# Seven products of sums for the gate/value matmuls of an mLSTM and SwiGLU kernel, in an order that a list scheduler writes

## The chip, the cores and the metric

The kernel runs on one core of a Trainium2 chip. The metric is the device time of one execution in microseconds (us). Five engines work side by side and meet at semaphores: TensorE (PE; its weight loads are listed as PEld), VectorE (DVE), ScalarE (ACT), GpSimd (POOL) and SyncE (SP), which here issues nearly all transfers. Each engine takes its instructions in program order.

## The reference

An mLSTM cell runs over 4 batches x 8 heads x 768 steps with head dimension 40. Its output, seen as 3072 tokens x 320 features, goes through a SwiGLU feed-forward block with 1536 hidden features. All in float32:

```python
for t in range(S):                                  # S = 768
    m_new = np.maximum(f[:, :, t] + m, i[:, :, t])
    f_stab, i_stab = np.exp(f[:, :, t] + m - m_new), np.exp(i[:, :, t] - m_new)
    m = m_new
    C = f_stab[..., None, None] * C + i_stab[..., None, None] * np.einsum('bhd,bhe->bhde', vt, kt)
    n = f_stab[..., None] * n + i_stab[..., None] * kt
    denom = np.maximum(np.abs(np.einsum('bhd,bhd->bh', n, qt)[..., None]), 1.0)
    y[:, :, t] = sigmoid(o_gate[:, :, t]) * np.einsum('bhde,bhe->bhd', C, qt) / denom
x = y.transpose(0, 2, 1, 3).reshape(3072, 320)
g = x @ w_gate                                      # 320 x 1536
out = (g * sigmoid(g) * (x @ w_val)) @ w_out        # 1536 x 320
```

## The kernel before, in words

The 768 steps are cut in six groups of 128. A group holds the 128 steps of all four batches, 512 tokens, and goes through three things: the cell (here always one group ahead), the gate/value products with the SwiGLU product, and the output projection. In the code g counts from 0, so "groups 3 to 6" are g = 2 to 5; group 2 is g = 1. The cell for group g + 1 runs inside group g's gate/value tiles; the last group, g = 5, has no cell to do.

**Gate/value.** `hidden(g, m)` makes one of 12 tiles of 128 hidden features. The transposed inputs `xT_sb` hold the 320 features as five chunks of 64 rows, twice: the upper 64 partitions feed the gate product and the lower 64 the value product, so that the two halves of TensorE's rows work at the same time. Line 651 issues, per chunk, one matmul of 64 rows x 128 features x 512 tokens for each half. ScalarE takes Silu of the gate's bank (`sg`, L656), VectorE multiplies by the value's bank into `h_sb` (L657). Float32 matmuls leave two records each in the trace.

**Cell.** Its steps stand in `slots[m]`, and are issued after tile m: `do_scores` (L331) and `do_weigh` after tiles 3 and 4, `do_add` (L353) and `do_state` after tile 5, `do_attend` (`inter` L377, `intra` L382) with `do_gather` for the two halves of the heads after tiles 7 and 9, `do_divide` after 8 and 10. `gather` makes `y_sb` and `den` on VectorE (L391, L394, then L396 to L398 on 16 columns); `gate` multiplies `o_sb` by it on GpSimd (L403); `divide` multiplies by 1/den on VectorE into `x_sb` (L409). `send_squares` (L422) moves x to `x_sq` in 32 transfers so that VectorE's 32x32 transpose (`turn_inputs`, L426) can write `xT_sb` while the projection runs. q and k come in the same way, 16 transfers each (`load_squares`, L315), into `q_sq` and a `k_sq` of its own. The weights of the next group (`weights_sub` L451, `weights_mask` L456, `weights_exp` L460, `sig` L463, `weigh_values` L341) are made during the projection.

**Projection.** In groups 2 to 6 `project_seven` already multiplies two 2x2 block matrices with seven products: halves of the tokens and of the hidden features against halves of `wo_sb`, with sums of inputs made by GpSimd (`out_sums`, L689 to L691) and of weights (`out_weights`, once). Each product is 12 matmuls of 128 x 128 x 160 columns (L717). Group 1 uses the plain `project_all` (L668).

**Order.** What runs when is written out by hand: tile m, its sums, its slot, and steps between the products of the projection. PSUM's eight banks rotate in two pools of four ("gen" for products, "cell" for the cell).

Of the kernel before, what the change touches and what calls it, by code (L numbers as in the profile page):

```python
# [9 lines left out]
F32 = mybir.dt.float32  # L10
# [8 lines left out]
L = 128  # L19
SUB = 64  # L20
NEG = -1e30


@with_exitstack
def kernel(
# [34 lines left out]
    NH = NFC + 1  # L60
# [6 lines left out]
    work = ctx.enter_context(tc.tile_pool(name="work", bufs=2))  # L67
    psum = ctx.enter_context(tc.tile_pool(name="psum", bufs=4, space=PSUM))
    early_scope = ExitStack()
    early = early_scope.enter_context(tc.tile_pool(name="early", bufs=1))  # L70
# [18 lines left out]
    k_sb = const.tile([128, BH, DP], F32)  # L89
# [7 lines left out]
    x_sb = const.tile([128, B, DM + HP], F32)  # L97
# [4 lines left out]
    h_sb = const.tile([128, NH, TW], F32)  # L102
# [3 lines left out]
    ident = const.tile([128, 128], F32)  # L106
# [498 lines left out]
    piece_load(3, h_sb[:, NH - NKC:])  # L605
# [68 lines left out]

    KH = NFC // 2
    NW = DM // 2
    TH = TW // 2
    first_half, second_half = slice(0, TH), slice(TH, TW)

    def out_weights(eng):  # L680
        lo, hi = wo_sb[:, 0:KH], wo_sb[:, KH:]
        n1, n2 = slice(0, NW), slice(NW, DM)
        eng.tensor_tensor(wT[:, 0], lo[:, :, n2], lo[:, :, n1], op=ALU.subtract)
        eng.tensor_tensor(wT[:, 1], hi[:, :, n2], wT[:, 0], op=ALU.subtract)
        eng.tensor_tensor(wT[:, 2], hi[:, :, n1], wT[:, 1], op=ALU.subtract)
        eng.tensor_tensor(lo[:, :, n2], hi[:, :, n2], lo[:, :, n2], op=ALU.subtract)

    def out_sums(k, eng):
        eng.tensor_tensor(S1[:, k], h_sb[:, k, second_half], h_sb[:, KH + k, second_half], op=ALU.add)  # L689
        eng.tensor_tensor(h_sb[:, k, second_half], h_sb[:, k, first_half], h_sb[:, k, second_half], op=ALU.subtract)  # L690
        eng.tensor_tensor(S2[:, k], S1[:, k], h_sb[:, k, first_half], op=ALU.subtract)  # L691

    def out_fourth(eng):
        for k in range(0, KH, 2):
            a12 = h_sb[:, KH + k:KH + k + 2, first_half]
            eng.tensor_tensor(a12, a12, S2[:, k:k + 2], op=ALU.subtract)

    def project_seven(g, before):
        n1, n2 = slice(0, NW), slice(NW, DM)
        a11 = lambda k: h_sb[:, k, first_half]  # L700
        a12 = lambda k: h_sb[:, KH + k, first_half]
        a21 = lambda k: h_sb[:, k, second_half]
        a22 = lambda k: h_sb[:, KH + k, second_half]
        node = {x: bank("o_ps", "gen")[:, 0:DM].rearrange("p (u d) -> p u d", d=NW) for x in "eacdb"}
        kept = {x: work.tile([128, TW], F32, name="sg")[:, 0:DM].rearrange("p (u d) -> p u d", d=NW) for x in "uv"}

        def send(z, u, n):
            for i in range(2):
                nc.sync.dma_start(out=out[ds((u + i) * S + g * L, L), n], in_=z[:, i])

        def fresh():
            return work.tile([128, DM], F32, name="z_sb").rearrange("p (u d) -> p u d", d=NW)

        def product(x, lhs, rhs, start, stop):
            for k in range(KH):
                for i in range(2):
                    nc.tensor.matmul(node[x][:, i], lhsT=lhs(k)[:, ts(i, L)], rhs=rhs(k), start=start and k == 0 and i == 0,  # L717
                                     stop=stop and k == KH - 1, skip_group_check=True)

        def step(n):  # L720
            for f in before.get(n, ()):
                f()

        u2, v = kept["u"], kept["v"]
        step(0)
        product("e", a12, lambda k: wo_sb[:, KH + k, n1], True, True)
        step(1)
        product("a", a11, lambda k: wo_sb[:, k, n1], True, True)
        nc.scalar.copy(u2, node["a"])  # L729
        z = fresh()  # L730
        nc.vector.tensor_tensor(z, u2, node["e"], op=ALU.add)  # L731
        send(z, 0, n1)
        out_fourth(nc.vector)
        step(2)
        product("c", a21, lambda k: wo_sb[:, k, n2], True, False)
        nc.scalar.copy(v, node["c"])
        step(3)
        product("d", lambda k: S1[:, k], lambda k: wT[:, 0, k], True, False)
        nc.vector.tensor_tensor(v, v, node["d"], op=ALU.add)
        step(4)  # L740
        product("b", lambda k: S2[:, k], lambda k: wT[:, 1, k], True, True)
        nc.vector.tensor_tensor(u2, u2, node["b"], op=ALU.add)
        nc.gpsimd.tensor_tensor(v, v, u2, op=ALU.add)
        send(v, 2, n2)
        step(5)
        product("c", a22, lambda k: wT[:, 2, k], False, True)
        z = fresh()
        nc.vector.tensor_tensor(z, u2, node["c"], op=ALU.add)
        send(z, 2, n1)
        step(6)  # L750
        product("d", a12, lambda k: wo_sb[:, KH + k, n2], False, True)
        nc.vector.tensor_tensor(u2, u2, node["d"], op=ALU.add)
        send(u2, 0, n2)
# [171 lines left out]
```

## Time and profile before

| | us |
|---|---|
| three runs, median (lowest to highest) | 537.33 (537.28 to 537.57) |
| span of the profiled execution, first to last instruction | 536.3 |
| its time outside the span, by the median of the runs | 1.0 |
| TensorE busy | 529.8 |
| VectorE, ScalarE, GpSimd busy | 261.0, 132.1, 182.4 |
| TensorE in gate/value products (L651), all groups | 317.2 |
| TensorE in the projection of groups 2 to 6 (L717) | 117.9 |
| first gate/value tile of group 2 starts | 125.1 |
| groups 2, 3, 4, 5 (start to start) | 83.3, 83.1, 83.2, 83.1 |
| group 6, to the end of its last matmul | 74.7 |

A row of a group of instructions reads: line, engine, operation, output <- inputs, shapes, count | busy time in us, mean ns of one | idle time of the engine ahead of them and what ended it. The chain in order of time is followed back from the last instruction to what released it; each row is start, duration, engine, tile and line. A row of busy time by engine gives a stretch, then TensorE, weight loads, VectorE, ScalarE and GpSimd, the granted clock (1.00 throughout), the share of the transfer engines and GB/s. A matmul's record outlasts the time after which the next can start, so periods are read from many in a row.

### The profile page before, as it was taken

To read this page: it belongs to the slowest core of one execution; us is meant where nothing else is said; L and a number is where in the kernel's file an instruction comes from. 1 tells how busy PE (TensorE), PEld (TensorE's weight loads), DVE (VectorE), ACT (ScalarE), POOL (GpSimd) and SP (SyncE) were. 2 spreads that over 40 slices of the span, in tenths; PEclk is the share of its full clock that TensorE was granted. 3 is DMA by queue.
4 is the path that set the end of the run, shared out by engine and by line. 5 is a ranking of instruction groups with operands and counts; after the bars stand their busy time and mean duration, and the time that the engine had idled before them with its cause. 6 is when DMAs were issued, how large, how long until landed. Compare 5 with 4: busy or idle time off the path is not lost.

```text
span 536.3 us, 12510 instructions
## 1 busy us (share of the span) xinstructions
PE 529.8 (99%) x5349; PEld 338.8 (63%) x5349; DVE 261.0 (49%) x437; ACT 132.1 (25%) x193; POOL 182.4 (34%) x194
## 2 busy tenths in 40 slices
PE   8999999999999999999999999999999999999997
PEld 4964545766745697555598455589455579544496
DVE  5769686982255542545633436635435734111121
ACT  3367555444110114101013210104201010011110
POOL 1303346579216534014627004437003530003410
PEclk9999999999999999999999999999999999999999
DMA  9999997898640496471296353296000131000001
GB/s 125 175 275 197 183 286 144 155 122 125 74 55 1 73 137 116 50 88 17 46 149 131 45 58 51 38 150 113 26 2 2 26 60 41 24 1 0 2 12 38
DMA packets 226879, 45.76 MB, mean 85 GB/s; under 512 B 214824, under 2 KB 221992, under 8 KB 226824
## 3 DMA queue, kind: packets, MB, share of 16 engines
q1 hardware_dynamic: 224916, 42.11, 48.9%
q10 hardware_dynamic: 1908, 2.85, 2.0%
q8 instruction: 42, 0.69, 0.6%
q14 instruction: 13, 0.11, 0.1%
HBM read 35.68 MB, written 4.01 MB: 74 GB/s over the span
## 4 chain that ended last, share of the span: by engine, by line
PE 91%; DMA 4%; SPq 3%; DVE 1%; POOL 0%; issue 0%; DVEq 0%; POOLq 0%
PE gv_ps L651 56%; PE o_ps L717 21%; PE o_ps L668 5%; SPq L117 3%; DMA wo_sb<-in_moe_w_gate_dram 2%; PE inter L377 2%; PE sp L331 2%; PE intra L382 2%; DMA raw<-in_moe_w_gate_dram 2%; PE add L353 2%; PE tp_kq L296 0%; POOL wgv_sb L207 0%; DVE M_sb L281 0%; PE tp_x L439 0%; DVE wgv_sb L200 0%
## 5 line engine op out<-in xcount | busy, mean ns | idle before, releaser
L651 PE MATMUL gv_ps<-xT,wgv_sb 64*128 64x512 f32 x1440 | 317.2, 593 | 0.9 <-DVE wgv_sb L207 0.8
L651 PEld LDWEIGHTS gv_ps<-xT,wgv_sb 64*128 64x128 f32 x1440 | 142.3, 187 | 155.2 <-issue 148.9
L657 DVE TENSOR_TENSOR h_sb<-sg,gv_ps 128x512 f32<-128x512 f32 x72 | 49.4, 686 | 177.3 <-ACT sg L656 177.3
L656 ACT ACTIVATE sg<-gv_ps 128x512 f32<-128x512 f32 x72 | 43.0, 597 | 264.8 <-PE gv_ps L651 264.6
L717 PEld LDWEIGHTS o_ps<-wo_sb,h_sb 128*128 128x128 f32 x480 | 65.6, 190 | 3.8 <-issue 3.8
L717 PE MATMUL o_ps<-wo_sb,h_sb 128*128 128x160 f32 x480 | 67.4, 300 | 0.0
L689 POOL TENSOR_TENSOR S<-h_sb 128x256 f32<-128x256 f32 x30 | 23.2, 773 | 100.9 <-DVE h_sb L657 100.9
L362 POOL TENSOR_TENSOR C<-C,dec 128x328 f32<-128x328 f32 x20 | 14.5, 736 | 114.6 <-DVE C L369 114.6
L456 POOL TENSOR_SCALAR_AFFINE_SELECT w_sb<-w_sb 64x1024 f32<-64x1024 f32 x20 | 28.4, 1421 | 37.1 <-DVE w_sb L451 36.1
L717 PE MATMUL o_ps<-wT,S 128*128 128x160 f32 x240 | 33.4, 299 | 0.0
L717 PEld LDWEIGHTS o_ps<-wT,S 128*128 128x128 f32 x240 | 32.9, 190 | 0.0
L668 PE MATMUL o_ps<-wo_sb,h_sb 128*128 128x320 f32 x96 | 26.9, 437 | 0.0
L690 POOL TENSOR_TENSOR h_sb<-h_sb 128x256 f32<-128x256 f32 x30 | 22.8, 760 | 2.4
L668 PEld LDWEIGHTS o_ps<-wo_sb,h_sb 128*128 128x128 f32 x96 | 17.9, 190 | 7.2
L691 POOL TENSOR_TENSOR S<-S,h_sb 128x256 f32<-128x256 f32 x30 | 21.7, 724 | 0.0
L394 DVE TENSOR_TENSOR y_sb<-y_sb,intra 64x328 f32<-64x328 f32 x40 | 19.7, 492 | 0.7
L369 DVE TENSOR_TENSOR C<-C,add 40x328 f32<-40x328 f32 (+1 forms) x36 | 17.7, 493 | 1.2 <-POOL C L362 0.6
L207 POOL TENSOR_TENSOR wgv_sb<-wgv_sb,low 128x640 int32<-128x640 int32 x6 | 9.3, 1544 | 24.6 <-DVE wgv_sb L200 24.6
L717 PE MATMUL o_ps<-wT,h_sb 128*128 128x160 f32 x120 | 17.1, 299 | 0.0
L731 DVE TENSOR_TENSOR z_sb<-sg,o_ps 128x320 f32<-128x320 f32 x5 | 2.4, 487 | 29.3 <-ACT sg L729 23.5
L426 DVE STREAM_TRANSPOSE xT<-x_sq 128x640 f32<-128x640 f32 x16 | 12.5, 822 | 8.5 <-DMA x_sq<-x_sb 8.5
L717 PEld LDWEIGHTS o_ps<-wT,h_sb 128*128 128x128 f32 x120 | 16.6, 190 | 0.0
(152 smaller groups left out, 471.8 us busy)
## 6 DMA issues: line engine op xcount, KB each, us to landing
w_sb<-M_dram SPq DMA_DIRECT2D x10, 512.0 KB, 11.3
x_sq<-x_sb SPq DMA_DIRECT2D x128, 40.0 KB, 2.0
k_sb<-in_k_dram SPq DMA_DIRECT2D x12, 320.0 KB, 6.0
v_sb<-in_v_dram SPq DMA_DIRECT2D x12, 320.0 KB, 5.8
o_sb<-in_o_gate_dram SPq DMA_DIRECT2D x12, 320.0 KB, 5.5
raw<-in_moe_w_out_dram SPq DMA_DIRECT2D x3, 1280.0 KB, 7.4
q_sb<-in_q_dram SPq DMA_DIRECT2D x32, 64.0 KB, 2.3
out_dram<-z_sb SPq DMA_DIRECT2D x20, 80.0 KB, 2.5
```

The costliest lines, as they stand in the source:

```text
L117: nc.sync.dma_start(out=dst[:, heads(P), 0:D], in_=tokens(a, c, P))
L369: nc.vector.tensor_tensor(c, c, ps[r], op=ALU.add)
L394: nc.vector.tensor_tensor(t, t, intra[i][half(c)], op=ALU.add)
L456: nc.gpsimd.affine_select(w, w, compare_op=ALU.is_ge, fill=NEG, base=0, pattern=[[0, UH], [1, SUB]], channel_multiplier=-1)
L651: nc.tensor.matmul(ps[i], lhsT=wgv_sb[half(i), m, PAIRS[kc][i] if g < 2 else kc, :], rhs=x[half(i), kc, :], start=(kc == 0), stop=(kc == N ...
L656: nc.scalar.activation(sg, ps[0], AF.Silu)
L657: nc.vector.tensor_tensor(hid(g, m), sg, ps[1], op=ALU.mult)
L668: nc.tensor.matmul(ps[u], lhsT=hid(g, m)[:, ts(u, L)], rhs=wo_sb[:, m, :], start=(m == 0), stop=(m == NFC - 1))
L689: eng.tensor_tensor(S1[:, k], h_sb[:, k, second_half], h_sb[:, KH + k, second_half], op=ALU.add)
L690: eng.tensor_tensor(h_sb[:, k, second_half], h_sb[:, k, first_half], h_sb[:, k, second_half], op=ALU.subtract)
L691: eng.tensor_tensor(S2[:, k], S1[:, k], h_sb[:, k, first_half], op=ALU.subtract)
L717: nc.tensor.matmul(node[x][:, i], lhsT=lhs(k)[:, ts(i, L)], rhs=rhs(k), start=start and k == 0 and i == 0, stop=stop and k == KH - 1, skip ...
```

## The change

Groups 3 to 6 no longer call `hidden`; `seven(g, m, t0)` takes its place. Four of the five chunks of a tile form a 2x2 block matrix (upper and lower rows of the tile's weights: value or gate, chunks 0-1 and chunks 2-3) that meets a 2x2 block matrix of inputs (chunks 0-1 and 2-3, first and second 256 tokens). The four results A, D (in bank `g*`) and B, E (in bank `v*`) come from seven products P1 to P7 of two chunks each, 64 rows x 128 x 256 columns, and four products of the fifth chunk (RA, RD, RB, RE): 18 matmuls, those of `g*` in one half of TensorE's rows and those of `v*` in the other; the halves swap with every tile. P1 is needed in both banks and P6's sum in two, so ScalarE copies bank to bank (`cA`), takes out P5 (`cP5`) and the sum U2 (`cU2`), and VectorE adds them into the banks (`joinD`, `joinE`), after which TensorE goes on adding products there. Silu and the SwiGLU product run on 256 columns, twice each.

```python
product("P1", r, ad, bA, rA, w[:, k1], x[:, k1, tok[0]], True, ["x0"])
product("P5", r, ad, bD, rD, Sj(1), x[:, k1, tok[1]], True, ["T1", sw(r, 1)])
W.add("A", 0.39, at("cA"), lambda: nc.scalar.copy(bB, bA), r=[rA], w=[rB, rE], banks=(ad, be))
product("P2", r, ad, bA, rA, w[:, k2], x[:, k2, tok[0]], need=["x0"])
product("RA", r, ad, bA, rA, w[:, rest], x[:, rest, tok[0]], need=["x0"])
W.add("A", 0.39, at("cP5"), lambda: nc.scalar.copy(P5[r], bD), r=[rD], w=[("P5", r)], banks=(ad,))
product("P6", s, be, bB, rB, Sj(0), Tx[:, 0], need=["T2", sw(s, 0)])
W.add("A", 0.39, at("cU2"), lambda: nc.scalar.copy(U2, bB), r=[rB], w=["U2"], banks=(be,))
W.add("V", 0.42, at("joinD"), tt(V, bD, U2, bD, ALU.add), r=["U2"], w=[rD], banks=(ad,))
product("P3", r, ad, bD, rD, Sj(2), x[:, k2, tok[1]], need=["x1", sw(r, 2)])
product("RD", r, ad, bD, rD, w[:, rest], x[:, rest, tok[1]], need=["x1"])
product("P7", s, be, bB, rB, w[:, k1], Tx[:, 1], need=["T3"])
W.add("V", 0.42, at("joinE"), tt(V, bE, P5[r], bB, ALU.add), r=[("P5", r), rB], w=[rE], banks=(be,))
product("P4", s, be, bB, rB, w[:, k2], Tx[:, 2], need=["T4"])
product("RB", s, be, bB, rB, w[:, rest], x[:, rest, tok[0]], need=["x0"])
product("RE", s, be, bE, rE, w[:, rest], x[:, rest, tok[1]], need=["x1"])
```

The sums of inputs (`Tx`, T1 to T4) are four VectorE operations of 128 x 512 a group, after the turn of x. The sums of weights (`Sw`) are made once, in group 2: per pair of tiles four sums on GpSimd, four on VectorE and four transfers between the partition halves, with two larger transfers at the start (`pair_weights`).

All of groups 2 to 6 is now added as tasks to a `Weave`, each with an engine, a planned duration, a priority time `at`, and the names it reads and writes. `run` simulates the engines with these durations and writes the program in that order:

```python
SLOT = 0.432
TO_PE, FROM_PE, CROSS, SWITCH = 0.1, 0.2, 0.06, 0.12
...
fit = sorted((tasks[i]["at"], i, r) for r, i in cands if r <= now + 0.1 and not clash(i, now))
...
first = fit[0]
if tasks[first[1]]["eng"] == "PE":
    picked = [first]
else:
    picked = [first]
    for x in fit[1:]:
        if tasks[x[1]]["eng"] not in ("PE", tasks[first[1]]["eng"]) and not set(tasks[x[1]]["banks"]) & set(tasks[first[1]]["banks"]):
            picked.append(x)
            break
```

So half-slots ("h0", "h1") go out in pairs of different halves and banks where a partner is ready, and cell blocks and halves of projection products ("PE") go out alone. Priorities: tile m of group g stands at T + 4.55 m with T = 78 (g - 1); scores, adds and three attends at T + (16, 19, 22, 25, 29, 34, 39); the projection at T + 54.

What else changes in groups 2 to 6:

```diff
-    psum = ctx.enter_context(tc.tile_pool(name="psum", bufs=4, space=PSUM))
+    psum = early_scope.enter_context(tc.tile_pool(name="psum", bufs=4, space=PSUM))
...
+    bk = {x: psum2.tile([128, 512], F32, name=x) for x in ("g0", "g1", "g2", "v0", "v1", "v2", "c0", "c1")}
...
-    k_sq = late.tile([128, PP, L // SQ, SQ], F32, name="k_sq")
+    k_sq = x_sq.rearrange("p w t d -> p (w t d)")[:, 0:PP * L].rearrange("p (a t d) -> p a t d", a=PP, d=SQ)
...
-        7: [run(weights_sub, 2, 1), run(weights_mask, 1), run(load_all, k_sb, k, 2)],
+        7: [run(weights_sub, 2, 1), run(weights_mask, 1)],
...
+    RANGES = ((0, 6), (6, 12), (12, 16))
...
+    NODE = dict(a="g0", c="c1", e="g1", d="c0", b="g2")
```

Tiles have three fixed bank pairs (`g0`/`v0` to `g2`/`v2`) and the cell two banks (`c0`, `c1`), which scores, adds and attends of each part take in turn; attend and gather run over 12, 12 and 8 heads (`RANGES`, in head pairs) for 16 and 16. `divide` writes into `o_sb`, from which x is sent. `k_sq` shares the memory of `x_sq`, so k's squares are fetched after x has been turned. k of group 3 is loaded at the start of group 2 and no longer during group 1's projection. The projection keeps its seven products with other sums: `S1` goes; per hidden tile GpSimd makes `half_sums` (6), `cross_sums` (6) and six sums for the fourth product, 18 a group as before; products run in the order a, c, e, d, b, c, d, each in two halves of six matmuls. Group 2's tiles (`plain`) are those of `hidden` on the new banks. Group 1 is as before.

## Prediction

> **What bounds the kernel now.** I read the page's first part and its costliest groups, then the chain in order of time, the same chain's groups 4 and 6, and last the engines that the change loads.
>
> ```profile
> PE 529.8 (99%) x5349; PEld 338.8 (63%) x5349; DVE 261.0 (49%) x437; ACT 132.1 (25%) x193; POOL 182.4 (34%) x194
> L651 PE MATMUL gv_ps<-xT,wgv_sb 64*128 64x512 f32 x1440 | 317.2, 593 | 0.9 <-DVE wgv_sb L207 0.8
> L717 PE MATMUL o_ps<-wo_sb,h_sb 128*128 128x160 f32 x480 | 67.4, 300 | 0.0
> ```
>
> TensorE is busy 99% of the span and waits 0.9 us in all for its gate/value inputs (L651); the 317.2 us of that line are what the change shortens. Nothing else ends late.
>
> ```profile
> 291.55 17.37 PE gv_ps L651 x80
> 308.91 2.02 PE sp L331 x128
> 310.94 8.78 PE gv_ps L651 x40
> 319.72 1.61 PE add L353 x120
> 321.33 8.78 PE gv_ps L651 x40
> 330.12 1.07 PE inter L377 x64
> 331.19 0.94 PE intra L382 x64
> 332.13 8.78 PE gv_ps L651 x40
> ...
> 351.72 23.02 PE o_ps L717 x168
> ...
> 457.84 51.70 PE gv_ps L651 x240
> 509.54 23.03 PE o_ps L717 x168
> ```
>
> This is one group (291.55 to 374.74, 83.2 us) and the last group, which has no cell. An f32 matmul leaves two records, and the two 64-row halves run side by side, so one tile m is 20 records in 10 pairs. Without interruptions it takes 51.70 / 12 = 4.308 us, a pair 430.8 ns. With a cell block between, two tiles take 8.78 us in place of 8.62: going to another tile shape of TensorE and back costs 0.16 us. Everything on this chain is TensorE, so a microsecond off its work is a microsecond off the time, as long as nothing else becomes late.
>
> **The change, part by part.** The sum starts from the profiled execution: span 536.3 us. The median of the three runs is 537.33, so 1.0 us lies outside the span; I carry it unchanged.
>
> *Seven products.* Of the five 64-row chunks of a tile, four go into seven products of two chunks, one stays with four products: 18 half-slots of 256 columns, nine pairs, where before it is the equivalent of ten. A pair slot (two passes) has no row at 256 columns; the nearest are these:
>
> ```profile
> 21.26 1.06 PE L519 MATMUL sp<-qT,kT 64*128 64x128 f32 x16
> ```
>
> Sixteen half-height matmuls of 128 columns are eight pairs: (1.06 - 0.272 of the last record) / 7 = 112.6 ns. Between 112.6 at 128 columns and 430.8 at 512, 256 columns come to 218.7 ns, a slot to 0.437 us, a tile to 9 x 0.437 = 3.936 us, 0.372 less. Groups 3 to 6 have 48 tiles: **-17.9 us**. Bounds: in proportion to columns (215.4 ns) -20.7; as two matmuls of 128 (225.2 ns) -12.2. I take the line between, since the full-height 160-column rows lie on it too (23.02 us / 168 = 137.0 ns, 139 by the line).
>
> The page "TensorE: Matmul & The Clock Gate" of the Trainium skill (Part 3, The mechanism) speaks against this: a weight load overlaps running matmuls only where the row group differs, and the section on LDWEIGHTS gives columns / 1.2 ns, an estimate of 107 ns for 128 columns. By that each pass would pay 107 ns more, some 1.9 us a tile, and the change would lose over 70 us. The 128-column rows refute it here: a full pass with its weight load every 112.6 ns, in both halves.
>
> *More switches of shape.* The cell is cut in seven TensorE blocks (two scores, two adds, three attends) for four, in four groups: 12 x 0.16 = 1.9 us. Project halves of 1.6 us that the list scheduler sets between half-slots add some more; together **+2.5** (1.9 to 5).
>
> *Unpaired halves.* A half-slot that finds no partner costs half a slot, 0.22 us. Two tiles give 10 + 8 half-slots to each row half, so they balance; at the start and end of a group partners are short. One or two a group: **+1.2** (0 to 5).
>
> *ScalarE copies and VectorE joins.* Per tile ScalarE gets five operations on 256 columns for one on 512. From the copy of 320 columns at 425 ns and those of 512 at 588, one is 0.37 us: 1.85 us for 0.60. VectorE gets four at about 0.42 (686 ns at 512, 487 at 320) for 0.69: 1.68. Both fit in a 3.9 us tile, but here the copy and joins stand between TensorE's own products: TensorE's queue runs in order, and behind a product that waits for its join stand the products of the next tiles. Three bank pairs and an order made from costs that agree with these rows (0.39, 0.42, slot 0.432) hide them; uncovered, one round trip is: last record outlasting its slot 0.16, to ScalarE 0.04, copy 0.37, back 0.04, weight load 0.11 = 0.72 us.
>
> What the planner's costs leave out shows in these answers (VectorE, then its own and GpSimd's clash):
>
> ```profile
> 291.50:374.70 83.20, 83.20 (x923) 53.12 (x922) 40.24 (x64) 16.00 (x22) 27.96 (x31) 1.00 0.54 80
> L397 DVE TENSOR_SCALAR den<-den x10: 176/1340/1348, 97.3 to 428.4; 128x16 f32<-128x16 f32 x10
> L409 DVE TENSOR_TENSOR x_sb<-o_sb,den x20: 428/484/1840, 103.7 to 432.2; 128x320 f32<-128x320 f32 x20
> L403 POOL TENSOR_TENSOR o_sb<-o_sb,y_sb x10: 1422/1426/1437, 100.7 to 428.3; 128x640 f32<-128x640 f32 x10
> ```
>
> In a group of 83.2 us VectorE is busy 40.2. It gains 12 x (1.68 - 0.69) = 11.9 for joins, four sums of x at 0.68 = 2.7, and a third gather, about 2: 57 of some 79 us, and most of the gathers stand in the stretch where joins are dense. The 16-column L397 takes 176 ns alone and 1340 when L403 runs on GpSimd, with which it starts in the same 0.1 us; L409 takes up to 1840 for 484. Planned are 0.2 and the bare length. With ranges of 12, 12 and 8 heads L403 is 1.07, 1.07 and 0.71 us, L397 up to 0.8, 0.8 and 0.4 late, and a multiply beside a GpSimd sum 0.53 each: up to 3.6 us a group, 10.8 in the three seven-product groups with a cell. In the kernel before this hid behind five idle microseconds of VectorE at a time; now a join stands behind it, and TensorE behind the join. What is late once moves TensorE and everything after it, so it is not paid twice. I take a third: **+3.5** (0 to 11).
>
> The Trainium skill's page "SBUF — State Buffer" (Who interferes with whom) has the rule: a VectorE instruction with two SBUF inputs, or in a two-port mode, and a GpSimd one exclude each other for the whole instruction. By it the joins (one input in PSUM) are free of this and the x sums are not; all of them blocked by a 0.75 us GpSimd sum would add an estimate of 2 to 3 us a group, which the sum does not hold.
>
> *SyncE and the group's end.* x goes out in 2 x 16 transfers, and k's squares now share x's buffer, so their 16 transfers start only when x has been turned. Before, the second batch of x of the group ahead of the one shown stood in the queue from 274.30 for 13.09 us, x was turned by 290.8 and TensorE used it at 291.55. The attends now stand some 9 us earlier (at 39 of 78 planned us for 49 of 83), which covers it; in group 2 about 24 moves of weight sums join the queue. GpSimd's 24 sums of 0.75 there are 18 us into a group of 83 where it has 40: covered, nothing of TensorE waits for them before group 3. **+1.0** (0 to 6).
>
> *At no cost.* The output sums on GpSimd stay 18 a group; k's earlier load moves to the group's start, needed 20 us later; the final VectorE sum and output after the last matmul stay.
>
> Sum: -17.9 + 2.5 + 1.2 + 3.5 + 1.0 = -9.7, so 537.3 - 9.7 = **527.6 us**.
>
> **Rivals.** *All waits are hidden*: only products and switches, -17.9 + 2.5: 521.9; with the lower bound of both, 518.5. For it: ScalarE and VectorE have room and the planner's figures are those of the rows. Against it: L397. *Round trips on the path*: the wait for joins replaces the product saved. It decides at (17.9 - 2.5) / 48 = 0.32 us a tile, under one half of the 0.72 us round trip; with 60% of the tiles showing one, 48 x 0.6 x 0.72 = 20.7, the time is 537.3 - 15.4 + 20.7 = 542.6, slower than before. For it: VectorE fuller, six waits of TensorE a tile where there were two, an order fixed beforehand. Against it: three tiles in flight, 11.8 us for a chain of about 8. *The halves do not run together*, so that it does not do what it says: with all 18 half-slots alone a tile takes 7.9 us, +170; two in 18 alone already cost the gain. Against it: in the rows above pairs keep together whatever their width, and the order alternates halves.
>
> **How the numbers follow.** A measurement can tell 0.2%, 1.1 us, from no change. My forecast, a part of the gain lost, has a chance of 0.46, with its own range 522.5 to 533; all hidden 0.27; round trips 0.17; lost pairs 0.04; a gain that is used up just so 0.06. Faster is 0.46 + 0.27 = 0.73, the same 0.06, slower 0.17 + 0.04 = 0.21. The range goes from the best case, 518.5, to 539, which holds the lower half of the round-trip case.
>
> **What would show it.** Right: gate/value pairs every 215 to 225 ns, groups 4 and 5 at 78 to 82 us, the last at 70 to 72, and TensorE's waits, a few tenths each, after VectorE's joins, bunched where L397's successor runs beside GpSimd. Group 2 stays near 83. The forecast is wrong if those waits reach 0.3 us a tile, if pairs take over 235 ns, or if x's turned inputs end the wait at a group's start by several microseconds.

## The result: slower by 3.5%

The changed kernel takes 556.59 us (median of 4 runs, 555.95 to 558.03) against 537.38 for the kernel before it in the same session (537.28 to 537.57): ratio 1.0348, 95% interval 1.0322 to 1.0374. The forecast was 527.6 us, faster. Its profiled execution took 557.16 us with a span of 555.4; the last matmul ends at 551.7 us, where before it was 532.6, so all of the loss, 19.2 us, lies between the start of group 2 (125.1 us in both) and that matmul.

The page of the changed kernel, its engines and, from the costliest groups, two of the gate/value lines (`mm` is now line 936, and every group of that line is one combination of tile names):

```profile
PE 535.3 (96%) x6117; PEld 427.1 (77%) x6117; DVE 334.3 (60%) x653; ACT 186.7 (34%) x385; POOL 204.2 (37%) x221
...
L936 PE MATMUL g<-xT,wgv_sb 64*128 64x256 f32 (+1 forms) x696 | 181.3, 422 | 8.0 <-ACT v L1009 5.8
...
L936 PE MATMUL v<-xT,wgv_sb 64*128 64x256 f32 (+1 forms) x312 | 112.9, 472 | 2.9 <-DVE v L939 2.9
```

TensorE's busy share falls from 99% to 96%, and behind the bar stand idle times that the kernel before did not have. "Busy" says little here, though: an instruction in one half of the rows counts as much as two side by side. Busy time by group (stretch, then TensorE, weight loads, VectorE, ScalarE, GpSimd, clock, transfers):

```profile
125.10:213.40 88.30, 84.66 (x921) 53.19 (x921) 52.27 (x95) 12.49 (x19) 50.45 (x55) 1.00 0.55 97
213.40:307.30 93.90, 88.08 (x1113) 78.31 (x1112) 58.78 (x114) 32.48 (x73) 38.61 (x40) 0.95 0.48 76
307.30:395.30 88.00, 83.98 (x1115) 75.79 (x1114) 55.49 (x112) 29.31 (x69) 29.11 (x32) 0.98 0.46 72
395.30:478.90 83.60, 82.48 (x1115) 74.09 (x1114) 49.80 (x111) 23.25 (x63) 18.49 (x24) 1.00 0.20 35
478.90:551.60 72.70, 72.70 (x601) 68.95 (x600) 23.75 (x56) 21.61 (x62) 13.75 (x19) 1.00 0.04 10
```

The same of groups 5 and 6 before, where TensorE is busy all the time:

```profile
374.70:457.80 83.10, 83.10 (x923) 53.02 (x922) 37.92 (x62) 10.03 (x16) 18.61 (x23) 1.00 0.14 30
457.80:532.60 74.80, 74.76 (x409) 45.97 (x408) 12.47 (x20) 8.01 (x14) 13.65 (x19) 1.00 0.03 10
```

Groups 2 to 5 take 88.3, 93.9, 88.0 and 83.6 us where they took 83.1 to 83.3; only group 6, which has no cell, gains (72.8 for 74.7, to the end of the last matmul). In groups 3 and 4 the granted clock is below 1. TensorE's longest waits from group 2 on (total, times, longest):

```profile
PE g L936 <- ACT v L1009: 5.8, 1, 5.8
PE v L936 <- DVE v L939: 2.9, 1, 2.9
PE g L936 <- DVE g L939: 2.2, 4, 0.7
PE g L936 <- ACT z_sb L799: 2.2, 1, 2.2
...
PE c L1060 <- DVE w_sb L939: 0.6, 2, 0.3
```

These are few, and most of their time is in two, not in one per tile. The products themselves are as forecast. TensorE in order of time, a stretch between two cell blocks of group 5 (start, duration):

```profile
416.85 0.38 PE L936 MATMUL v<-Tx,wgv_sb 64*128 64x256 f32 x1
416.85 0.38 PE L936 MATMUL v<-Tx,Sw 64*128 64x256 f32 x1
417.06 0.38 PE L936 MATMUL v<-Tx,wgv_sb 64*128 64x256 f32 x1
417.07 0.38 PE L936 MATMUL v<-Tx,Sw 64*128 64x256 f32 x1
...
418.79 0.38 PE L936 MATMUL v<-Tx,Sw 64*128 64x256 f32 x1
418.79 0.38 PE L936 MATMUL v<-Tx,wgv_sb 64*128 64x256 f32 x1
```

The two halves start within 10 ns of each other, and nine steps of a pair take 418.79 - 416.85 = 1.94 us, 215.6 ns each (218.7 were assumed). Elsewhere, late in group 3:

```profile
288.89 0.70 PE L936 MATMUL v<-xT,wgv_sb 64*128 64x256 f32 x2
289.42 1.02 PE L936 MATMUL v<-Tx,wgv_sb 64*128 64x256 f32 x4
290.29 0.59 PE L936 MATMUL v<-xT,wgv_sb 64*128 64x256 f32 x2
290.81 0.40 PE L936 MATMUL g<-wo_sb,h_sb 128*128 128x160 f32 x1
```

From 289.42 six records of one half follow each other at the same pace, with nothing beside them: the other half is idle for 1.3 us, and no view calls that a wait.

So I counted, from the records of all matmuls after 125.1 us, how long both halves (or a full-height matmul) work, a cell block, one half alone, or nothing; each pass is taken at its full-clock length, so time lost to a halved clock falls under "nothing":

| us from 125.1 to the last matmul | both | cell | one half | nothing | sum |
|---|---|---|---|---|---|
| before | 370.9 | 27.9 | 1.1 | 7.5 | 407.5 |
| after | 338.5 | 27.8 | 27.2 | 33.1 | 426.6 |
| of it groups 2, 3, 4, 5, 6 | 74.2, 63.9, 66.3, 66.8, 67.3 | 7.1, 6.9, 6.9, 6.9, 0 | 0.2, 11.0, 6.4, 5.3, 4.3 | 6.8, 12.0, 8.4, 4.6, 1.3 | |

Work done with one half alone counts half. The products saved (370.9 + 0.5) - (338.5 + 13.6) = 19.3 us; lone halves cost 13.6 - 0.5 = 13.1; "nothing" (waits, switches of shape, lost clock) grew by 25.6. Together +19.4, the loss within the rounding.

### The profile page after: what moved, and what is told of

It reads as the page before. It is cut to its first block, busy times and chain, and to the rows that moved or that the text cites. A ratio compares the mean times of both kernels' runs of the same rounds, so it can differ in the third digit from the quotient of the medians.

```text
span 555.4 us, 14660 instructions
## 1 busy us (share of the span) xinstructions
PE 535.3 (96%) x6117; PEld 427.1 (77%) x6117; DVE 334.3 (60%) x653; ACT 186.7 (34%) x385; POOL 204.2 (37%) x221
## 4 chain that ended last, share of the span: by engine, by line
PE 54%; SPq 10%; DVE 7%; DMA 3%; issue 2%; ACT 1%; POOL 0%; DVEq 0%; ACTq 0%
PE g L936 28%; PE v L936 14%; PE c L936 7%; SPq L1165 4%; SPq L1048 4%; DVE y L939 2%; SPq L1174 2%; DMA Sw<-wgv_sb 1%; PE c L1060 1%; PE c L1083 1%; PE c L1068 1%; PE c L1088 1%; DVE den L1112 1%; DMA x_sq<-o_sb 1%; DVE Tx L939 1%
## 5 line engine op out<-in xcount | busy, mean ns | idle before, releaser
L936 PE MATMUL g<-xT,wgv_sb 64*128 64x256 f32 (+1 forms) x696 | 181.3, 422 | 8.0 <-ACT v L1009 5.8
L936 PEld LDWEIGHTS g<-xT,wgv_sb 64*128 64x128 f32 x696 | 116.7, 190 | 39.9 <-issue 25.2
L936 PE MATMUL v<-xT,wgv_sb 64*128 64x256 f32 (+1 forms) x312 | 112.9, 472 | 2.9 <-DVE v L939 2.9
L936 PE MATMUL g<-xT,Sw 64*128 64x256 f32 x384 | 95.2, 386 | 2.2 <-DVE g L939 2.2
L936 PE MATMUL v<-Tx,wgv_sb 64*128 64x256 f32 x384 | 90.8, 389 | 0.0
L936 PEld LDWEIGHTS g<-xT,Sw 64*128 64x128 f32 x384 | 63.6, 187 | 6.7 <-DVE g L939 3.8
L936 PEld LDWEIGHTS v<-Tx,wgv_sb 64*128 64x128 f32 x384 | 63.6, 191 | 3.8 <-ACT U L1014 0.3
L936 PEld LDWEIGHTS v<-xT,wgv_sb 64*128 64x128 f32 x312 | 55.3, 188 | 6.2 <-DVE v L939 3.7
L789 PE MATMUL gv_ps<-xT,wgv_sb 64*128 64x512 f32 x240 | 53.3, 594 | 0.3 <-DVE wgv_sb L345 0.3
L789 PEld LDWEIGHTS gv_ps<-xT,wgv_sb 64*128 64x128 f32 x240 | 23.6, 187 | 24.8 <-issue 23.8
L936 PEld LDWEIGHTS c<-wo_sb,h_sb 128*128 128x128 f32 x240 | 33.1, 190 | 1.7 <-issue 1.0
L936 PEld LDWEIGHTS c<-wT,h_sb 128*128 128x128 f32 x240 | 33.1, 190 | 0.0
```

The lines of the kernel that those rows point to most:

```text
L789: nc.tensor.matmul(ps[i], lhsT=wgv_sb[half(i), m, PAIRS[kc][i] if g < 2 else kc, :], rhs=x[half(i), kc, :], start=(kc == 0), stop=(kc == N ...
L936: nc.tensor.matmul(out_ap, lhsT=lhsT, rhs=rhs, start=start, stop=True, skip_group_check=True)
```

## Theories

**Theory A** has two parts. First, the list scheduler's own order leaves TensorE unused: on its own planned durations the plan ends 403.6 us after its first task, with 50 half-slots alone (10.8 us) and 64 planned switches between half-slots and other work of TensorE (7.7). The kernel before took 407.5 us for the same stretch, so on paper only 3.9 us were gained. Second, on the chip TensorE ends 23.0 us later than that plan, in few steps: queues that run in order stood behind transfers whose planned costs are too small, and a wait of some microseconds also halves the clock. **Rival B**: copies and joins stand on TensorE's path in every tile, the "round trips" of the prediction. **Rival C**: VectorE and GpSimd clash, the prediction's own term, with a larger price.

Against B speaks the lateness of each TensorE instruction against its planned time: it is 2.2 us at the start, 5.9 at 80 us of the plan, jumps by 7.9 around 217 us (trace time) and by 4.5 around 318, and is nearly flat between, while each tile has its three copies and two joins.

**The stall at 217 us.** SyncE's queue, GpSimd and ScalarE in order of time (start, duration, engine; in brackets idle time and its releaser):

```profile
195.27 13.24 SPq L1165 DMA_DIRECT2D x_sq<-o_sb  x16
208.57 1.76 SPq L255 DMA_DIRECT2D o_sb<-in_o_gate_dram  x2
210.38 3.44 SPq L968 DMA_DIRECT2D Sw<-Sw  x4
```

```profile
214.53 3.22 POOL L939 TENSOR_TENSOR Sw<-wgv_sb,Sw 64x256 f32<-64x256 f32 x4 [6.62 <-DMA Sw<-Sw]
217.71 1.15 POOL L1186 TENSOR_SCALAR_AFFINE_SELECT w_sb<-w_sb 64x1024 f32<-64x1024 f32 x1
```

```profile
218.88 1.06 ACT L598 ACTIVATE w_sb<-w_sb 128x1024 f32<-128x1024 f32 x1 [11.09 <-POOL w_sb L1186]
219.96 1.28 ACT L601 ACT_TABLE_LOAD   x1
221.25 1.36 ACT L601 ACTIVATE o_sb<-o_sb 128x640 f32<-128x640 f32 x2
222.52 0.90 ACT L1009 COPY v<-g 128x256 f32<-128x256 f32 x3
```

Read from the bottom up. TensorE waits for the copies of line 1009, `cA` of group 3's first tiles. They need only a finished product, but stand in ScalarE's queue behind the exponential of the next weights, which waited 11.09 us for GpSimd's mask. The mask stands behind the last sums of weights, which waited 6.62 us for the moves `Sw<-Sw`, and those stand in SyncE's queue behind 16 transfers of x. At three places of the chain the link is a queue and not data: the copies need no weights, the mask needs no sums, the moves need no x.

**The stall at 318 us** is shorter and, by the same reading, of the same make: SyncE, then VectorE:

```profile
308.00 8.53 SPq L1048 DMA_DIRECT2D x_sq<-in_k_dram  x16
```

```profile
318.35 2.37 DVE L1123 STREAM_TRANSPOSE kT<-x_sq 128x1024 f32<-128x1024 f32 x2 [3.56 <-DMA out_dram<-sum_v]
...
320.95 0.42 DVE L939 TENSOR_TENSOR v<-P,v 128x256 f32<-128x256 f32 x1
```

k's squares now share x's buffer, so they are fetched at the start of the group, and VectorE waits for them ahead of the transpose with the joins queued behind it (the releaser that the row names is the transfer that came last, not the one needed). No run below changes k's squares alone, so this chain is read from the queues and not shown.

**The clock.** Busy time and granted clock (third number from the right) in and after the two stalls:

```profile
217.00:218.00 1.00, 0.12 (x1) 0.00 (x0) 0.00 (x0) 0.00 (x0) 0.97 (x2) 1.00 0.66 69
218.00:222.00 4.00, 0.00 (x0) 0.00 (x0) 0.00 (x0) 3.09 (x4) 3.92 (x4) 0.58 0.67 76
222.00:223.00 1.00, 0.06 (x1) 0.06 (x1) 0.49 (x1) 1.00 (x3) 0.31 (x1) 0.50 0.66 76
...
227.00:228.00 1.00, 1.00 (x8) 0.96 (x6) 0.08 (x1) 0.87 (x3) 0.00 (x0) 0.50 0.57 171
228.00:229.00 1.00, 1.00 (x8) 0.96 (x7) 0.77 (x2) 0.37 (x1) 0.00 (x0) 0.55 0.36 28
...
320.00:321.00 1.00, 0.00 (x0) 0.00 (x0) 1.00 (x3) 0.00 (x0) 0.00 (x0) 1.00 0.50 109
321.00:322.00 1.00, 0.58 (x2) 0.50 (x4) 0.68 (x3) 0.61 (x2) 0.17 (x1) 0.53 0.69 77
...
323.00:324.00 1.00, 1.00 (x8) 0.91 (x5) 0.43 (x1) 0.12 (x1) 0.00 (x0) 0.50 0.53 53
324.00:325.00 1.00, 1.00 (x10) 0.88 (x9) 0.00 (x0) 0.06 (x1) 0.00 (x0) 0.77 0.08 17
```

After the wait of 5.8 us TensorE works at half the clock from 222.9 to beyond 228, and lateness grows by another 3.0 us; after the one of 2.9 us from 321.4 to 324.5, another 1.4. The clock falls while TensorE still waits: by the 0.58 of the row from 218 to 222 it was at half from about 218.6 (an estimate from that mean), 1.5 us after TensorE stopped at 217.1. The Trainium skill ("TensorE: Matmul & The Clock Gate", Part 1) says the clock falls to half after an idle window of some 3.4 us and comes back after as long a busy one. By it the second wait should have cost nothing more. The rows decide: 2.9 us was enough here, and from TensorE's first work to the full clock it took 3 us once and 6 the other time.

## Experiments

"Plan" is the end of the scheduler's own simulation, counted from its first task; "drift" is how much later the last matmul of the profiled execution comes: its end less 125.1 less the plan.

| kernel | us, median (range) | ratio to before (95%) | plan | drift |
|---|---|---|---|---|
| after | 556.59 (555.95 to 558.03) | 1.0348 (1.0322 to 1.0374) | 403.6 | 23.0 |
| e1 plain tiles | 544.45 (543.84 to 546.11) | 1.0133 (1.0110 to 1.0156) | 404.2 | 8.7 |
| e2 no copies, no joins | 546.48 (546.15 to 552.41) | 1.0187 (1.0134 to 1.0240) | 403.6 | 12.3 |
| e3 measured transfer costs | 548.22 (547.17 to 549.90) | 1.0196 (1.0174 to 1.0219) | 404.4 | 14.9 |
| e4 old bank pools | 557.54 (556.12 to 559.87) | 1.0371 (1.0336 to 1.0406) | 403.6 | 22.0 |
| e5 multiply planned later | 553.38 (550.74 to 553.75) | 1.0278 (1.0247 to 1.0308) | 402.5 | 20.3 |
| e6 no weight-sum moves | 548.62 (546.26 to 549.38) | 1.0196 (1.0170 to 1.0221) | 403.6 | 14.1 |
| e7 priorities searched | 539.17 (536.34 to 540.58) | 1.0024 (1.0007 to 1.0040) | 391.4 | 17.0 |
| e8 costs and priorities | 530.11 (529.71 to 533.14) | 0.9871 (0.9842 to 0.9900) | 393.5 | 9.1 |
| e9 e8's planner, plain tiles | 541.82 (541.49 to 541.98) | 1.0072 (1.0057 to 1.0087) | 404.2 | 6.7 |
| e10 e8 with e5's edit | 534.49 (531.33 to 534.81) | 0.9913 (0.9883 to 0.9943) | 392.4 | 11.4 |
| e11 denominators first | 551.03 (548.58 to 551.81) | 1.0237 (1.0207 to 1.0268) | 404.6 | 16.1 |
| e12 e8 with e11's edit | 529.91 (528.59 to 532.62) | 0.9862 (0.9830 to 0.9894) | 392.8 | 9.3 |

**e1: the scheduler alone.** Groups 3 to 6 keep plain tiles in the new order.

```diff
-            (plain if g == 1 else seven)(g, m, t0)
+            plain(g, m, t0)
```

> Only the list scheduler, without the seven products: groups 3 to 6 take the plain tiles that group 2 has, the sums of weights and of x are gone; banks, cell, projection and task order by the scheduler stay. The planner's own schedule for it ends at 404.2 us from its first task, that of the changed kernel at 403.6. Theory A (the order leaves halves of TensorE unpaired, so that on paper already the products gain nothing, and a few stalls where an engine's queue stands behind a transfer make the rest): 540 us, 537 to 545, since the stalls of 6 us at 217 and 3 us at 318 need copies, joins and moves of weight sums that are not here. Theory B (TensorE waits for copies and joins all along, 0.3 to 0.7 us a tile): about 537 to 540 as well, so this run does not part A from B. Theory C (the list scheduler's cell order costs the time, whatever the products): 552 or more.

544.45 us. The new order alone costs some 7 us, and the seven products in this order make it 12 worse. The two plans end within 0.6 us of each other, but they do not count alike. The planner charges a switch of shape only between half-slots and other work of TensorE; plain tiles are entered as "PE" like the cell and the projection, so e1's plan charges none, after's 64 (7.7 us). In e1's trace the shape changes 65 times in groups 2 to 6 (41 times before, 79 in after); at the planner's 0.12 us that is 7.8, and on equal terms the products save some 8 us on paper. From group 2 on, e1 has one wait worth a row:

```profile
PE g L936 <- ACT z_sb L799: 2.2, 1, 2.2
```

The other 6.5 us of its drift come without a wait, a little in every group, as uncharged switches would.

**e2: no copies and joins.** The same program order, with 240 instructions left out.

```diff
-        W.add("A", 0.39, at("cA"), lambda: nc.scalar.copy(bB, bA), r=[rA], w=[rB, rE], banks=(ad, be))
+        W.add("A", 0.39, at("cA"), None, r=[rA], w=[rB, rE], banks=(ad, be))
```

> The changed kernel in exactly its program order, with the three ScalarE copies and two VectorE joins of each tile left out (240 instructions; the sums in the banks are then not those of the reference). TensorE's instructions are the same and stand in the same order. Theory A: the waits for copies and joins are hidden in the steady state; only what stands behind the stalls at 217 and 318 us comes forward in part: 547 to 554. Theory B (round trips of 0.72 us on most of the 48 tiles): 20 to 35 us less, 522 to 537.

546.48 us: 10 less than after, and 9 more than before. With every round trip gone, the kernel is still slower than before, and B's band is not reached. TensorE then waits elsewhere:

```profile
PE g L936 <- ACT sg L1027: 6.8, 3, 4.4
```

That is Silu, in the same queue of ScalarE. Even with these 6.8 us added to the 10, the rival's 20.7 us of round trips were not there. That 10 us went, half a microsecond more than A's band allows, fits A: what stood in the queues behind the transfers were these copies and joins, and without them fewer half-slots are left alone (17.4 us in place of 27.2 by the same count).

**e3: the planner's costs for transfers.** Only durations and delays of SyncE's tasks are set to those of the trace of after, and SyncE starts 4.2 us late, as it did.

```diff
+        free["S"] = 4.2
-        W.add("S", 0.7, t0 + r, lambda r=r: nc.sync.dma_start(
+        W.add("S", 1.6, t0 + r, lambda r=r: nc.sync.dma_start(
-        w=[("xsq", P, t, r)], lag=2.2)
+        w=[("xsq", P, t, r)], lag=2.6)
...
```

> Only the planner's costs of transfers are changed to what the trace shows (SyncE begins 4.2 us late; 0.72 us for a move of x in place of 0.62, 0.54 for squares, 2.2 for weights, 1.0 for other loads, later landings), so the order on ScalarE, VectorE, GpSimd and SyncE comes out another; the work is the same. Its planned end is 404.4 (403.6 before). Theory A: queues are no longer caught behind transfers, so the stalls and the halved clock after them go, some 12 to 16 us: 541 to 545. Theory B: the plan's end is what it was and waits for copies remain: 553 to 557.

548.22 us, 8.4 less although the plan is 0.8 longer, but less than I said. The stall at 217 us is gone; a step of 2 us at 177 us of the plan, where after has its stall at 318, stays. Since the whole order of the other engines moved with the costs, this run alone does not show that transfers were the cause; e6 does for the first stall.

**e4: the bank pools of group 1.** In after, the new pool makes TensorE wait 2.2 us for `z_sb` at the start of group 2.

```diff
-    bk = {x: psum2.tile([128, 512], F32, name=x) for x in ("g0", "g1", ..., "c1")}
+    bk = {x: bank(x, tag) for tag, names in (("cell", ("g0", "v0", "g1", "v1")), ("gen", ("g2", "v2", "c0", "c1"))) for x in names}
```

> Only the eight banks of groups 2 to 6 are taken from the PSUM pools that group 1 uses, slot by slot, and not from a new pool that takes the old ones' place. All theories: group 2's first product no longer waits 2.2 us for group 1's last result copy, so 554.4, or nothing at all where the later SyncE queue takes it back: 553.5 to 556.6.

557.54 us, no gain and a microsecond above the band. The wait at the start is gone and is paid 25 us later, where the cell's scores wait 2.4 us for VectorE's `w_sb`, which stands in its queue behind sums of weights that wait for transfers: a start earlier than the transfers gains nothing.

**e5: GpSimd's multiply later.** Its task names `den` as read.

```diff
-        W.add("G", na * 0.18, at + 0.9, tt(G, o, o, y[:, :, 0:D], ALU.mult), r=ys, w=[("o", ra)])
...
+        W.add("G", na * 0.18, at + 0.9, tt(G, o, o, y[:, :, 0:D], ALU.mult), r=ys + [("den", yi)], w=[("o", ra)])
```

> The changed kernel with GpSimd's multiply of the gather put behind VectorE's three small operations on the denominators, so that the 16- to 24-column operation that lasted 1.0 us beside it runs alone; the division then waits for GpSimd. The planned end is 402.5 for 403.6. The prediction's term (lateness of VectorE beside GpSimd reaches TensorE, 3.5 us): 552 to 553. Theory A (the plan has slack there, and TensorE's lateness against the plan grew by only about 0.6 us in the gathers of groups 4 and 5): 554.5 to 556.5.

553.38 us, between the two bands, 3.2 less than after, of which 1.1 is the plan. But it is no test of the clash: the edit only moves the instruction in the program, and GpSimd's multiply needs no data of the denominators. VectorE and GpSimd of e5, in order of time:

```profile
170.96 0.98 DVE L1111 TENSOR_SCALAR den<-den 128x12 f32<-128x12 f32 x1
```

```profile
170.79 1.12 POOL L939 TENSOR_TENSOR o_sb<-o_sb,y 128x480 f32<-128x480 f32 x1 [1.71 <-DVE y L939]
```

They still run together, and the operation on 12 columns still takes 0.98 us. What the run does show is that stalls shift by microseconds even with so small a change of order (the step of lateness at 217 us is 1.8 in place of 4.8, the one at 318 us 4.3 in place of 3.1).

**e6: no moves of weight sums.** The 26 transfers of `Sw` are left out and `Sw` is zero.

```diff
+    nc.vector.memset(Sw, 0.0)
-            W.add("S", 0.7, t0 + 3, lambda r=r, s=s: nc.sync.dma_start(out=slot(r, 1), in_=slot(s, 2)), ...)
+            W.add("S", 0.7, t0 + 3, None, ...)
```

> The changed kernel in its program order without the 26 transfers of weight sums between the partition halves in group 2; the memory they would fill is set to zero once (one VectorE operation at the start of group 2), so the seven products of groups 3 to 6 are not those of the reference. Theory A (the wait of 6.0 us at 217 us is a chain: SyncE's queue, move of a weight sum, GpSimd's sum, GpSimd's mask behind it, ScalarE's Exp and Sigmoid, the copy behind them, TensorE; and the 2.5 us at 150 to 157 are VectorE's sums behind the first two moves): both go, and the halved clock after the first, 9 to 12 us: 545 to 548. If instead ScalarE is just too full at a group's start: 554 to 557.

548.62 us, 8.0 less, half a microsecond short of A's band. The delay near 150 us and the stall at 217 us are gone, as the reading of the chain says. The one at 318 us stays (2.5 us of lateness), so the moves have no part in it:

```profile
PE v L937 <- DVE v L940: 2.3, 1, 2.3
```

**e7: another order of the same tasks.** Only the priorities change, found by a random search over the planner's own simulation with its own costs. Its plan has no lone half-slot.

```diff
-AT = {(name, r): 0.91 * x for name, x in AT.items() for r in range(2)}
-CELL = (16, 19, 22, 25, 29, 34, 39)
+AT = {("cA", 0): 30.697, ("P1", 0): -1.371, ...}
+CELL = (-2.05, 22.23, -96.91, 11.76, 22.1, 19.8, 24.75)
```

> Only the priorities are changed: the 40 values of AT, the seven of CELL, and the times of loads, projection and weights, searched so that the planner's own schedule with its own costs ends at 391.4 in place of 403.6. Tasks, engines and amounts of work are the same. Theory A (TensorE follows the planned schedule, so what the plan leaves unpaired is lost on the chip one to one, and stalls at transfers come on top): 12 us less if the stalls stay as they are, 544; 538 to 548. Theory B (copies and joins are what TensorE waits for): a fuller plan has less slack for them, no gain or a loss: 554 or more.

539.17 us, 17.4 less than after, in A's band: 12.2 of it is the plan. One half alone works 1.4 us in place of 27.2, both 351.4. The copies and joins are all still there, so Theory B's "no gain or a loss" is refuted.

**e8: costs and order together.** e3's costs, slightly longer ones for GpSimd's sums and for the way to TensorE, the banks of e4, a cost for each table load and for the exclusion of VectorE and GpSimd, and priorities searched on these.

```diff
+                d = tasks[i]["us"]
+                if tasks[i]["table"] and tasks[i]["table"] != table:
+                    d, table = d + 1.28, tasks[i]["table"]
+                if tasks[i]["port"]:
+                    d += max(0.0, free["G"] - s)
```

> The changed kernel's tasks with four changes to the plan alone: transfer costs as in the third run of the first call, table loads charged at the operation that changes the table, VectorE operations with two SBUF inputs and GpSimd's excluding each other, banks as in the fourth run; and the priorities searched for these costs. The planned end is 393.5, with 4 half-slots alone where the changed kernel's plan has 50. Theory A: TensorE ends 4 to 9 us later than planned (125.1 us of group 1 before it, some 5 after it): 528 to 533, faster than the kernel before. Theory B: 553 or more.

530.11 us: faster than both kernels, by 1.3% than before. The page of e8 and TensorE's longest wait:

```profile
PE 521.7 (98%) x6117; PEld 411.1 (77%) x6117; DVE 335.7 (63%) x653; ACT 189.1 (36%) x385; POOL 204.2 (38%) x221
```

```profile
PE c L1079 <- DVE C L950: 2.4, 1, 2.4
```

The same number of matmuls as in after, 24 us shorter in the stretch. In the count above: both 351.6, cell 28.1, one half 3.4, nothing 19.5, sum 402.6. Which of the new costs makes the 9 us between e7 and e8 is not shown, since all came at once. The wait of 2.4 us, from 151.9 us on, for the cell's state on VectorE, again halved the clock:

```profile
155.00:156.00 1.00, 1.00 (x29) 0.82 (x22) 0.97 (x3) 0.00 (x0) 0.00 (x0) 0.50 0.10 16
```

The profiled execution is the slowest of the four (533.14 us, mean clock 0.995; the others 529.71 to 530.29 at 0.999 or 1.0), so the count is of a slower execution than the median.

**e9: e8's planner with plain tiles.** Is that the products, or just a better planner? The costs and banks are those of e8; the priorities are not e8's searched ones but those of after.

```diff
-            (plain if g == 1 else seven)(g, m, t0)
+            plain(g, m, t0)
```

> The planner with the measured costs of transfers and table loads, the excluded port and the old bank pools, as in e8, but with plain tiles in groups 3 to 6 (no sums of weights or inputs, no copies and joins; the output is complete). Its plan ends at 404.2 us, with TensorE never idle in it, against 393.5 in e8. Theory A (the products of sums are worth what the plan says, once the order can use them): the plan is nearly all TensorE work, so little can drift; e1 less the stalls that the costs take away, 536 to 540 us, that is 7 to 10 more than e8. Rival B (e8's gain over the kernel before came from the scheduler and its costs, not from the products): within 2 us of e8, 528 to 532.

541.82 us, 1.8 above what A gave, and slower than before by 0.7% (ratio 1.0072). So Rival B is refuted: with the products the planner's kernel is 11.7 us faster than without, and without them it loses to the order written by hand. Part of the 11.7 may be the search of the priorities, which only e8 had. TensorE has nothing to wait for in e9, so a search could save only switches, some 3 us if it came down to the 41 of before:

```profile
125.10:536.00 410.90, 410.90 (x4090) 257.48 (x4088) 168.91 (x302) 64.20 (x94) 126.42 (x146) 1.00 0.34 57
```

Busy all the time and still 6.7 us behind its plan: as in e1, the plan charges none of its 65 switches. Both 371.1, cell 27.6, one half 1.1, nothing 11.2 (7.5 in the order written by hand). e8 against that: 18.3 us of work saved (lone halves counted half), 1.2 given back in lone halves and 8.3 in switches and waits, 8.3 to the good in the two profiled executions.

**e10: e8 with e5's edit.**

> e8 with GpSimd's multiply of each gather placed after VectorE's denominators, as in e5, and the priorities searched anew (plan 392.4 us against 393.5). Theory A (e8's planner already counts the excluded port, so e5's gain can't be had twice): only the 1.1 us of the plan, 528 to 531 us. Rival B (the clash still cost e8 what it cost the changed kernel, some 2 us beside the plan): 525 to 528 us.

534.49 us (531.33 to 534.81): no gain over e8 but 4.4 us more, outside both bands. It has e5's flaw: the clash was not removed. It shows only that a plan shorter by 1.1 us need not be a faster kernel.

**e11: the clash really removed.** VectorE multiplies by 1/den first, and GpSimd's multiply by y needs its result.

```diff
-        W.add("G", na * 0.18, at + 0.9, tt(G, o, o, y[:, :, 0:D], ALU.mult), r=ys, w=[("o", ra)])
         W.add("V", na * 0.09 + 0.1, at + 1.2, tt(V, o, o, den.to_broadcast([128, 2 * na, D]), ALU.mult), r=[("den", yi)], w=[("o", ra)])
+        W.add("G", na * 0.18, at + 1.3, tt(G, o, o, y[:, :, 0:D], ALU.mult), r=ys, w=[("o", ra)])
```

> The changed kernel with the two multiplies of the gather swapped: VectorE multiplies o by 1/den first, then GpSimd multiplies the same data by y, so that GpSimd's multiply really waits for the denominators on the chip (in e5 only the program's order changed, and the multiply still ran beside them, 170.79 beside 170.96 us). Its plan ends at 404.6 us against 403.6. The one-microsecond rows of the denominators should go to about 0.2 us. Theory A (the clash costs TensorE about what the two visible steps of 0.6 us at gathers show): 555 to 558 us, no measurable gain. Rival B (the forecast's term of 3.5 us is really paid): 551.5 to 554.5 us with the plan's 1.0 counted.

The denominator's operation in after and in e11 (shortest/median/longest ns, first and last start):

```profile
L1112 DVE TENSOR_SCALAR den<-den x12: 172/981/1033, 171.0 to 444.5; 128x12 f32<-128x12 f32 x8, 128x8 f32<-128x8 f32 x4
```

```profile
L1111 DVE TENSOR_SCALAR den<-den x12: 171/173/657, 170.6 to 438.1; 128x12 f32<-128x12 f32 x8, 128x8 f32<-128x8 f32 x4
```

It falls from 981 to 173 ns, and the kernel takes 551.03 us, 5.6 less although the plan is 1.0 longer, below the band of rival B. The median of 981 agrees with the Trainium skill ("SBUF — State Buffer", Who interferes with whom): one of the two engines stands still for the other's whole instruction (GpSimd's takes 1.1 us). Not all of the 5.6 us need be the clash itself: the stalls at 217 and 318 us are 1.5 and 1.3 us shorter here, each with less clock lost behind it, and e5 showed that these shift with the clash still there.

**e12: the same in e8.**

> e8 with the same swap and the priorities searched again for it (plan 392.8 us against 393.5). Theory A: 528.5 to 532 us, as e8. Rival B (the clash with GpSimd is what makes e8 drift): 525 to 528 us.

529.91 us (528.59 to 532.62), as e8: in that order the clash is worth nothing that shows. Both are the fastest, and the runs do not tell them apart.

## Why the prediction was wrong

The sign was wrong. The 25.6 us by which "nothing" grew are, by lateness, 2.2 at the start of group 2, 2.9 near 150 us, 7.9 and 4.5 at the two stalls; the rest, some 8, is switches of shape and small steps. By the prediction's own steps:

- **Seven products, -17.9: right.** Measured -19.3 in after, and -18.3 in e8 against e9; a pair takes 215.6 ns, in proportion to the columns, the better of the two bounds. The rival that the halves do not run together, with the lowest chance (0.04), is refuted as a matter of the hardware, but its condition, that two lone half-slots in 18 already cost the gain, named what went wrong as a matter of order: 27.2 us with one half alone are 63 half-slots of 0.431 us, 1.3 in the 18 of each tile.
- **Unpaired halves, +1.2 (0 to 5): the step that failed first.** It is +13.1. I argued that two tiles give 10 + 8 half-slots to each half, "so they balance". A balance over two tiles does not put partners side by side: the scheduler takes the first ready half-slot and looks for a partner only among what is ready at that moment. Its plan has 50 lone half-slots, 10 to 18 a group. e7, with the same copies and joins, has 1.4 us of lone halves in place of 27.2, so it was the priorities that left them, and its 12.2 us of shorter plan came through on the chip.
- **SyncE and the group's end, +1.0 (0 to 6): the second.** I asked whether each moved transfer lands before it is needed and found slack. I did not ask what stands behind each waiting instruction in the in-order queues of GpSimd, ScalarE and VectorE. The stalls at 217 and 318 us cost 7.9 and 4.5 us with their clock, the delay near 150 us 2.9. e6 (-8.0) shows that the moves of weight sums time the first and the delay; for the stall at 318 us the link to k's squares is only read from the queues. I named the weight-sum moves and wrote "covered": TensorE did not wait for the sums, but for what stood behind the mask, which began only at 217.71 us, after the last of them.
- **VectorE and GpSimd, +3.5 (0 to 11): of the right size, not by the path described.** Removing the clash gives 5.6 us in after (e11) and nothing in e8 (e12). Most of what e11 gains stands at the two stalls and not in the gathers, where a join was to hold TensorE up.
- **Switches, +2.5 (1.9 to 5): somewhat low.** With plain tiles, e9's stretch is 410.9 us against 407.5, so the finer cut of the cell, 65 changes of shape for 41, costs 3.4 without any product. After has 79; at the same price a change, an estimate of 5.4.
- **Round trips on the path, the rival that came out on the right side: right sign (542.6 us), wrong mechanism.** It would need a wait in 60% of the tiles; the view of waits shows nine in its five rows, six of them after copies and joins, in all of groups 2 to 6, and e2 without any copies is still slower than before. I had set as a sign that the waits after joins "reach 0.3 us a tile"; the six sum to 10.9 us, 0.23 a tile, but 8.7 of it is two waits and not a cost of each tile.
- **At no cost: group 2 "stays near 83".** It took 88.3, since its start waits for `z_sb` and the weight sums delay the cell's scores.

What stays open: about 9 us of drift in e8 and e12, which no run took apart (in e8 some 7 of it arise in group 2's first 40 us, in steps of 1.3, 3.0 and 1.0, the last two at the wait of 2.4 us and the halved clock behind it; the rest comes in small steps later); what starts the stall at 318 us; and how much of e11's gain is the clash alone.

## What to carry to other kernels

A saving in TensorE work that needs two halves is worth what the order can pair: count the lone halves in the order that is written, since no view of a profile calls them idle. When an order comes from a planner, first read the end of its own plan against the time of the stretch it replaces (here 403.6 against 407.5 us); what it lacks on paper the chip did not give here. Compare two plans only if both charge the same things: these left the switches of shape out for plain tiles. And for each instruction that waits for a transfer, read down its queue: the cost of a late transfer is what stands behind it, and not only what needs it.

## What the hardware showed that I had not expected

- Waits of 2.4 us (e8) and 2.9 us already halved TensorE's clock, the second for 3.1 us of work; one of 5.8 us for 6. So the price of the two stalls of after was about half as much again (1.4 on 3.1, 3.0 on 4.8).
- Pairs of 64-row matmuls keep 215 ns or so at 256 columns also with their starts shifted by half a pass (in after, one half starts at 272.42, 272.64, 272.85 and 273.07 us, the other at 272.54, 272.75, 272.97 and 273.19). A half alone goes no faster (289.42 us), so a missing partner costs half a slot.
- Changing only the order of the program (e7) moved the same instructions from 556.59 to 539.17 us, and small changes of order shift single stalls by 2 to 3 us either way.
